# Attention with a gated MLP on one core: the half-size first product in step 0 of both blocks

## The chip, the cores and the metric

The kernel runs on one core of one Trainium2 chip. The time is device microseconds of one execution. Three runs of the kernel before gave 706.75, 707.27 and 707.87 us; the median, 707.27, is the time before.

The engines are called by the profile's names: PE is TensorE's matmul, PEld its weight load, DVE is VectorE, ACT is ScalarE, POOL is GpSimd, SP is SyncE, which here only issues DMAs.

## The reference

For x of 2048 x 1024 (bf16), with 32 heads of 32 and a hidden width of 3584:

```python
xn = _layernorm(x)
s = _A_ref(xn, A_wqkv, A_wo)           # attention of each position to 8 positions, 2 apart, then @ wo
g = _silu(_B_ref(xn, B_w1, B_w3, B_w2))
return x + s * g

def _B_ref(x, w1, w3, w2):
    gate = jnp.einsum("bsd,df->bsf", x, w1)
    up = jnp.einsum("bsd,df->bsf", x, w3)
    h = _silu(gate) * up
    return jnp.einsum("bsf,fd->bsd", h, w2)
```

## The kernel before

**Blocks, chunks, steps.** The 2048 rows are worked in two blocks of 1024, and each block in two chunks of 512 columns of the transposed x. A block goes through the q, k and v products (`qkv_pairs`), the gate/up steps (`up_step`, 14 of them, each for 256 of the 3584 hidden columns), the down product (`mlp_down`) and the output product (`wo`). The attention itself (`scores`, `softmax`, `values`) is DVE work that is spread between these. The output product of the first block's second chunk runs inside block 1, between its v products and its first steps; its output tile is stored from one of the six large buffers ("r8").

**Seven products for eight.** Each product is a 2 x 2 block product done with seven products instead of eight (the Strassen-Winograd form). For the gate/up step the four block operands of x are the two chunks times the two halves of the contraction (`bx`), their sums are `tx`, made once a block by `xn_sums` into the tile `xs`. The weights are blocked as gate (w1) and up (w3) times the two halves of the contraction; their four sums are made by `w_sums` (line 1307) in block 0, stored in DRAM (`s_dram`), and loaded again in block 1 as "st." (`up_load`, line 1216). A full product of a step is, for each of two groups of 128 hidden columns, four matmuls of 128x128 weights by 512 columns. `mm` (line 586) issues them at line 593.

**The half-size form.** The first of the seven products (w1's first half with the first chunk's first half) has no sums in it. In steps 1 to 13 it is itself done in the 2 x 2 form, with blocks of half the size: `up_first` (line 1267), seven pairs of matmuls of 256 columns, issued at line 1283. Its weight sums are made by `w_sums2` (line 1237: three DVE instructions named wss0, wss2 and wss3) in block 0, stored (`s2_dram`, POOL's queue) and loaded in block 1 ("s2.", SP's queue) into the part of the weight tile that w3's first half would take. Its x sums are made once a block by `x_sums2` (line 1253: four DVE instructions, named xt) into the place of xT's second chunk, first half, which nothing reads any longer. Between the pairs stand copies on ACT (`ufork`, `us5p`, `usnap`) and one DVE sum inside PSUM (`ucc`). `up_first` is a generator: `up_step` (line 1321) of the step before draws its four parts one after the other between its own products, so that the copies and the sum have time. The rows `L2F` (line 497) say which steps take this form; step 0 does not, since no step stands before it: it does the first product as two groups of four matmuls of 512 columns.

**What sets the order.** Nothing runs in program order. Every operation is first recorded with a cost and a due time (`Plan.op`). `Plan.listed` (line 254) makes a list for each engine from these, and then moves single operations by the table `ORDER` (line 328): a pair (a, b) takes operation a out and puts it right behind b; one row of the table for each of PE, DVE, ACT, POOL and SP. Each engine, and each DMA queue, then works strictly in its list's order, and waits for what its next operation needs. Operations are known in the table by their running number, so an added operation renumbers all behind it.

Vector sums are issued at line 602 (`tt`), copies at 607 (`cp`), silu at 624, DMAs at 634; the groups of the profile are told apart by their tiles and shapes. In the profile "r" is one of the six large buffers, "k" an SBUF tile for partial results, "mm" a PSUM bank, "a" an attention tile, "h_sb" the hidden activations.

Of the kernel before, what the change touches and what calls it, by code (L numbers as in the profile page):

```python
# [42 lines left out]
class Plan:  # L43
# [420 lines left out]
def kernel(  # L464
# [29 lines left out]
    L2B = (0, 1)  # L494
    LKB, EKB = 200, 200
    RL = (0,1,2)
    L2F = {0: range(1, 14), 1: range(1, 14)}
    KEEP = ('l1', 'l2')
    U2B = (0,1)
    CH_ = [r.split() for r in ("turn1_2_1 put_sq0_0", "ofork0_1 exp1", "u2_l10_1 sq2", "fk_l10_1 var2_1")]  # L500
# [806 lines left out]
    def w_sums(fb):  # L1307
# [9 lines left out]
        if U2B and fb:  # L1317
            w_sums2(fb)
# [780 lines left out]
```

## Time and profile before

| | us |
|---|---|
| median of 3 runs | 707.27 (706.75 to 707.87) |
| the profiled execution | 707.13 |
| its span, first to last instruction | 705.4 |
| PE busy | 696.8 |
| DVE busy | 676.4 |
| ACT busy | 385.4 |
| POOL busy | 40.6 |

The granted TensorE clock was 1.00 throughout. The span is 1.7 us shorter than the execution that it was taken from. Busy times say how much of the span an engine had an instruction in work; PE's are modelled, since its matmuls overlap. So the distance from one start to the next is the better measure of PE, and a list of waits the better measure of what held it. Times inside the profile are counted from the span's start. In this execution the first block's gate/up steps begin shortly after 81 us, and block 1's near 425 us.

### The profile page before, as it was taken

The page shows a single profiled execution, that of the slowest core. Times are in us where ns is not written, and L with a number is a line of the kernel's source. Part 1 is how long each engine was busy: PE and PEld are TensorE (multiplying, and loading weights), DVE is VectorE, ACT ScalarE, POOL GpSimd, SP SyncE. Part 2 cuts the span into 40 slices and gives each one's busy share as a digit, 9 for nine tenths or more (in the row PEclk, how much of TensorE's full clock was granted, in tenths as well). Part 3 has the DMA queues.
Part 4 walks back from the last instruction along what each step waited for, and adds up shares of the span by engine and source line. Part 5 has one row for each costly group of instructions (what it writes and reads, how often), then busy time and mean ns, then how long its engine had stood idle before and what let it go on. Part 6 is the DMA issues. An engine that isn't in the chain of part 4 may idle for free.

```text
span 705.4 us, 9790 instructions
## 1 busy us (share of the span) xinstructions
PE 696.8 (99%) x3611; PEld 374.5 (53%) x3666; DVE 676.4 (96%) x831; ACT 385.4 (55%) x752; POOL 40.6 (6%) x83
## 2 busy tenths in 40 slices
PE   9999999999999999999999999999999999999997
PEld 5555555545545474744555554454555555656443
DVE  8889999999999999999979999999999999999877
ACT  6644465658465796812564454566756755222143
POOL 1001020012101000000010000000100010000000
PEclk9999999999999999999999999999999999999999
DMA  9998889787788899996776767976675668858403
GB/s 333 291 354 305 300 290 319 256 271 268 227 300 291 300 287 212 300 270 215 266 240 237 238 212 225 306 240 217 204 237 177 199 187 251 270 210 268 153 28 119
DMA packets 142351, 174.06 MB, mean 247 GB/s; under 512 B 16912, under 2 KB 117280, under 8 KB 135648
## 3 DMA queue, kind: packets, MB, share of 16 engines
q1 hardware_dynamic: 131408, 138.10, 62.0%
q0 software_dynamic: 6240, 33.84, 12.8%
q10 hardware_dynamic: 4656, 1.51, 1.0%
q8 instruction: 28, 0.46, 0.3%
q14 instruction: 19, 0.16, 0.1%
HBM read 117.31 MB, written 43.78 MB: 228 GB/s over the span
## 4 chain that ended last, share of the span: by engine, by line
PE 94%; DVE 3%; DMA 2%; issue 1%; SPq 0%; ACT 0%; DVEq 0%; ACTq 0%
PE mm L593 82%; PE mm L1554 6%; PE mm L1283 5%; DMA r<-s_dram 1%; DVE r L602 1%; DVE a L602 1%; DMA r<-in_A_x_dram 1%; DMA out_dram<-r 1%; PE mm L781 0%; DVE small L699 0%; SPq L634 0%; DVE r L715 0%; DVE xT L602 0%; DVE E L602 0%; ACT k L607 0%
## 5 line engine op out<-in xcount | busy, mean ns | idle before, releaser
L593 PEld LDWEIGHTS <-r 128*128 128x128 f16 (+1 forms) x2068 | 219.6, 108 | 192.0 <-DMA r<-in_A_wqkv_dram 0.5
L593 PE MATMUL mm<-xs,r 128*128 128x512 f16 x1280 | 305.2, 379 | 0.3 <-DMA r<-s_dram 0.2
L593 PE MATMUL mm<-xT,r 128*128 128x512 bf16 (+2 forms) x747 | 177.6, 369 | 2.1
L607 ACT COPY k<-mm 128x512 f32<-128x512 f32 (+1 forms) x226 | 121.0, 565 | 74.0 <-PE mm L593 54.0
L607 ACT COPY mm<-mm 128x512 f32<-128x512 f32 (+1 forms) x157 | 75.6, 487 | 117.0 <-DVE mm L602 36.1
L593 PE MATMUL mm<-r,h_sb 128*128 128x512 f16 (+1 forms) x581 | 130.1, 379 | 0.6
L593 PEld LDWEIGHTS <-h_sb 128*128 128x128 f16 (+1 forms) x680 | 66.6, 98 | 78.4
L602 DVE TENSOR_TENSOR a<-a 128x2048 bf16<-128x2048 bf16 (+7 forms) x106 | 106.7, 1011 | 0.3
L602 DVE TENSOR_TENSOR h_sb<-mm,k 128x1024 bf16<-128x1024 f32 x48 | 58.2, 1217 | 7.1 <-PE mm L593 3.9
L1283 PE MATMUL mm<-xT,r 128*128 128x256 f16 (+1 forms) x364 | 61.1, 273 | 0.0
L602 DVE TENSOR_TENSOR a<-qo,kT 128x2048 bf16<-128x2048 bf16 x48 | 57.5, 1218 | 0.3 <-ACT kT L607 0.2
L602 DVE TENSOR_TENSOR h_sb<-h_sb 128x1024 f16<-128x1024 bf16 (+7 forms) x74 | 55.0, 748 | 0.2
L1283 PEld LDWEIGHTS <-r 128*128 128x128 bf16 (+1 forms) x364 | 35.6, 98 | 32.0
L602 DVE TENSOR_TENSOR a<-E,vT 128x2048 bf16<-128x2048 bf16 x42 | 50.3, 1217 | 0.3 <-issue 0.3
L602 DVE TENSOR_TENSOR k<-mm,k 128x1024 f32<-128x1024 f32 (+1 forms) x44 | 44.8, 1023 | 2.2 <-PE mm L593 2.1
L624 ACT ACTIVATE k<-k 128x512 bf16<-128x512 f32 x56 | 34.7, 636 | 15.5 <-DVE k L602 15.4
L602 DVE TENSOR_TENSOR r<-r,r 128x1024 f16<-128x1024 f16 (+7 forms) x56 | 42.5, 768 | 0.1
L624 ACT ACTIVATE h_sb<-mm 128x512 bf16<-128x512 f32 x60 | 36.2, 611 | 5.7 <-PE mm L593 5.5
L602 DVE TENSOR_TENSOR qo<-qo,a 128x2048 bf16<-128x2048 bf16 x32 | 39.0, 1219 | 0.3
L602 DVE TENSOR_TENSOR r<-r 128x1024 f16<-128x1024 bf16 (+4 forms) x71 | 36.1, 515 | 0.2
L602 DVE TENSOR_TENSOR h_sb<-h_sb,k 128x2048 bf16<-128x2048 bf16 x28 | 34.1, 1218 | 1.3 <-ACT k L607 1.2
L607 ACT CAST k<-mm 128x512 bf16<-128x512 f32 x56 | 32.3, 598 | 0.9 <-PE mm L593 0.7
(129 smaller groups left out, 528.9 us busy)
## 6 DMA issues: line engine op xcount, KB each, us to landing
r<-in_B_w_dram SPq DMA_DIRECT2D x42, 512.0 KB, 5.4
s_dram<-r POOLq DMA_DIRECT2D x14, 1024.0 KB, 5.2
r<-s_dram SPq DMA_DIRECT2D x14, 1024.0 KB, 5.7
r<-t_dram SPq DMA_DIRECT2D x15, 896.0 KB, 6.8
r<-in_A_wqkv_dram SPq DMA_DIRECT2D x10, 1024.0 KB, 8.6
r<-in_B_w_dram SPq DMA_DIRECT2D x11, 896.0 KB, 5.6
h_sb<-in_B_w_dram SPq DMA_DIRECT2D x14, 512.0 KB, 6.8
t_dram<-h_sb POOLq DMA_DIRECT2D x7, 1024.0 KB, 6.3
```

The source lines that it names most:

```text
L593: nc.tensor.matmul(cut(ps.ap()), lhsT=lhs[k](), rhs=cut(rhs[k]()), start=(first and k == 0), stop=(last and k == n - 1), skip_group_check= ...
L602: plan.op(DVE, name, lambda: fn(out=o(), in0=a(), in1=b()), rd, wr, occ, 0.08, late=late)
L607: plan.op(ACT, name, lambda: nc.scalar.copy(out=o(), in_=a()), rd, wr, occ, 0.11)
L624: plan.op(ACT, name, lambda: nc.scalar.activation(out=o(), in_=a(), func=ACTF.Silu), rd, wr, occ, 0.11, table="silu")
L1283: nc.tensor.matmul(half(pa[i].ap, n)(), lhsT=A[0][k](), rhs=B[0][k](), start=first and k == 0, stop=k == 1, skip_group_check=True)
L1554: nc.tensor.matmul(half(bank.ap, n)(), lhsT=a[k](), rhs=c[k](), start=first and k == 0, stop=k == NQ - 1, skip_group_check=True)
```

## The change

Step 0 of both blocks does its first block product in the half-size form, as steps 1 to 13 do. For that

- `L2F` takes in step 0;
- `up_step` of step 0 goes through `up_first` of its own step at once, before its other products are recorded;
- block 0 makes the weight sums of `w_sums2` for step 0 too, and stores them; block 1 loads them ("s2.0");
- `x_sums2` of block 0 is recorded ahead of `w_sums(0)` instead of behind it, with no other change; in block 1 it stays behind the scores;
- the table `ORDER` is another one for all five engines.

In the built kernel PE has 16 matmuls of 512 columns less and 28 of 256 more; DVE has 5 instructions more (three weight sums, two sums in PSUM), ACT 6 copies more, POOL one store and SP one load more. The lists that both kernels share differ in many places: 82 of PE's 907 shared operations stand out of their old sequence, 200 of DVE's 828, 234 of ACT's 727, 79 of SP's 259 and 22 of POOL's 70. PE's list is the same up to 57 us of the old trace and from 597 us on; DVE's and ACT's differ from 14 us to the end.

```diff
 ORDER = (
...
-    L2F = {0: range(1, 14), 1: range(1, 14)}
+    L2F = {0: range(0, 14), 1: range(0, 14)}
...
             dma(SP, f"w3.{fb}", lambda: wv()[:, 1, KH:KT], lambda: w3_r[:, KH:KT, fc], [], [(wt, 1, 1)], 256)
-            if b in U2B and fb:
+            if b in U2B:
                 dma(SP, f"s2.{fb}", lambda: s2_v(wt).rearrange("p q k n -> p (q k n)"),
                     lambda: s2_dram[fb].rearrange("p q k n -> p (q k n)"), [("sd2", fb)], [(wt, 1, 0)], 256)
...
-        if U2B and fb:
+        if U2B:
             w_sums2(fb)
...
         more = up_first(b, fb + 1) if fb + 1 in L2F[b] else iter(())
+        if two and not fb:
+            for _ in up_first(b, fb):
+                pass
         pa, pe, pb = [PA[b, fb] if two and x == "a" else banks(*(f"u{x}{b}_{fl[i]}" for i in I)) for x in "aeb"]
...
         if b == 0:
+            x_sums2()
             w_sums(0)
...
         if b:
             scores(c0)
-        if b in U2B:
+        if b:
             x_sums2()
```

In the changed lists, PE's last quarter of block 0's new product stands behind the first product with sums of step 0 (`ue0`) and ahead of the last v products. The sum `ucc` that it needs stands on DVE right behind the second pair sum of the v products (`qc22`). In block 1, DVE's new `ucc` stands among the sums of the first block's second output chunk, and SP's stores of that chunk stand in another sequence.

262 rows, old and new, of the table ORDER are left out of this document.

## The prediction

> **What bounds the kernel now.** I read the page's first lines, then what TensorE (PE) waits for, then the chain of waits, because the change touches PE work and the question is whether PE time is the kernel's time.
>
> ```profile
> span 705.4 us, 9790 instructions
> ...
> PE 696.8 (99%) x3611; PEld 374.5 (53%) x3666; DVE 676.4 (96%) x831; ACT 385.4 (55%) x752; POOL 40.6 (6%) x83
> ```
>
> ```profile
> PE mm L575 <- DVE k L573: 1.3, 1, 1.3
> PE mm L781 <- DVE r L715: 0.3, 1, 0.3
> PE mm L593 <- DMA r<-s_dram: 0.2, 1, 0.2
> ```
>
> PE is busy 99%, VectorE (DVE) 96%. A busy PE is a modelled figure, so the second fence matters more: in the whole execution only three waits of PE are listed, 1.8 us in all, and two of them are in the first microseconds. The chain of waits tells how fast PE issues when nothing holds it; its columns are start, length and what, with the count of matmuls:
>
> ```profile
> 630.31 3.02 PE mm L593 x14
> 633.33 7.64 PE mm L1554 x70
> ```
>
> 14 matmuls of 512 columns in 3.02 us are 215.7 ns each; 70 of 256 columns in 7.64 us are 109.1 ns each. So PE is a full queue with hardly a hole, and work taken from it shortens the kernel one for one, unless something else then arrives last. Two things might: DVE, and one DMA.
>
> DVE first. The columns of the windows are the stretch, its length, then busy time and instruction count of PE, PEld, DVE, ACT and POOL, then clock, DMA share and GB/s.
>
> ```profile
> 50.50:83.60 33.10, 32.94 (x152) 18.94 (x154) 32.49 (x36) 13.41 (x26) 2.12 (x4) 1.00 0.85 301
> 58.00:362.00 304.00, 302.79 (x1574) 161.93 (x1596) 301.69 (x395) 183.44 (x347) 24.96 (x47) 1.00 0.84 272
> 410.00:452.00 42.00, 41.74 (x204) 20.83 (x205) 41.76 (x49) 21.77 (x46) 1.09 (x2) 1.00 0.76 239
> ```
>
> In the first block, 58 to 362 us, DVE is busy 301.69 of 304 us: it works off a backlog, and what PE needs is merely placed early enough in it. The backlog is empty for the first time at 362 us, where DVE idles 3.12 us:
>
> ```profile
> 361.95 0.42 DVE L602 TENSOR_TENSOR xT<-xT 128x512 f16<-128x512 bf16 x1
> 365.49 1.23 DVE L602 TENSOR_TENSOR h_sb<-mm,k 128x1024 bf16<-128x1024 f32 x1 [3.12 <-ACT k L607]
> ```
>
> The DMA is the third wait of PE, and the chain shows what stands behind it:
>
> ```profile
> 436.34 1.14 DVE a L602
> 437.48 0.61 DVE r L602
> ...
> 439.54 3.61 DMA out_dram<-r
> ...
> 443.20 8.90 DMA r<-s_dram
> ...
> 452.15 3.63 PE mm L593 x16
> ```
>
> ```profile
> 451.35 0.60 PE L1283 MATMUL mm<-xT,r 128*128 128x256 f16 x4
> 452.15 1.04 PE L593 MATMUL mm<-xs,r 128*128 128x512 f16 x4 [0.20 <-DMA r<-s_dram]
> ```
>
> In block 1 the load of step 2's weight sums (st.2) needs a buffer that holds the output of the first block's second chunk. The last sums of that output leave DVE at 438.09, the last of its stores is issued at 439.54 and lands at 443.15, then the load takes 8.90 us. PE's four half matmuls of 451.35 end their issue at 451.35 + 4 x 0.109 = 451.79, and PE starts again at 452.15: it stands still for 0.36 us. Whatever PE gains before 452 us counts only as far as st.2 comes sooner too.
>
> **The change, part by part.** *PE work.* In each block's step 0 two accumulations of four 512-column matmuls go, 8 per block, 16 in all; seven pairs of 256-column matmuls come, 14 per block, 28 in all. 16 x 215.7 = 3.451 us against 28 x 109.1 = 3.055 us: 0.40 us less, half of it in each block. The Trainium skill, page "TensorE: Matmul & The Clock Gate", section "Back-to-back issue gap", speaks against this: it gives streams of weight load and matmul about 81 ns for 128 columns and 131 ns for 512. By that (estimate) 28 half products would cost at least 28 x 81 = 2.27 us against 16 x 131 = 2.10, a loss of 0.17 us or more; the trace disagrees with its 215.7 ns, so the measurement decides.
>
> *DVE.* Three new weight sums for step 0 (block 0 only: block 1 loads them), and one combining sum in PSUM per block.
>
> ```profile
> 83.54 1.28 DVE L602 TENSOR_TENSOR r<-r 128x1024 f16<-128x1024 bf16 x2
> ...
> 85.88 0.41 DVE L602 TENSOR_TENSOR r<-r 128x512 f16<-128x512 bf16 x1
> 86.22 1.21 DVE L602 TENSOR_TENSOR a<-a 128x2048 bf16<-128x2048 bf16 x1
> 87.35 0.28 DVE L602 TENSOR_TENSOR r<-r 128x256 f16<-128x256 bf16 x1
> 87.55 1.21 DVE L602 TENSOR_TENSOR a<-a 128x2048 bf16<-128x2048 bf16 x1
> ...
> 95.97 0.68 DVE L602 TENSOR_TENSOR mm<-mm,k 128x512 f32<-128x512 f32 x1
> 96.57 0.41 DVE L602 TENSOR_TENSOR r<-r 128x512 f16<-128x512 bf16 x1
> ```
>
> From start to next start the same sums of step 1 take 0.34, 0.20 and (same form) 0.20 us, the combining sum 0.60. So block 0 gets 0.74 + 0.60 = 1.34 us more and block 1 0.60 us. Over block 0 the 1.34 us fit the 3.12 us hole at 362 us; without that cover they would cost 1.34. The x sums are only moved: the same four instructions.
>
> *Step 0 of block 0 itself.* Now the last quarter of the half-size product waits for the combining sum. On DVE, in the order of the changed kernel, it stands right behind the second sum of the v products, after which the next instruction starts at 83.54 today; ahead of that sum stand the same instructions plus the three weight sums. So it starts between 83.54 + 0.74 = 84.28 and, if the idle 33.10 - 32.49 = 0.61 us closes, 83.67, and gives its result 0.69 us later: 84.36 to 84.97. PE:
>
> ```profile
> 81.56 1.67 PE L593 MATMUL mm<-xT,r 128*128 128x512 bf16 x7
> 83.07 2.75 PE L593 MATMUL mm<-xs,r 128*128 128x512 f16 x12
> ```
>
> The old product ends at 83.07 (8 matmuls, one record missing), the eight behind it 1.73 us later, 84.80. In the changed order the same work stands ahead of the last quarter, less 8 x 0.2157 plus 12 x 0.1091: 84.38. So PE stalls 0 to 0.6 us. I take 0, the near end, since DVE's idle time there is mostly waiting for PE sums that now have other work in front; 0.6 stays in the range. Behind the waiting matmul stands all of PE, so the price is full.
>
> *ScalarE* gets three 256-column copies per block. Each takes about as long as this group's mean (the third number):
>
> ```profile
> L607 ACT COPY mm<-mm 128x256 f32<-128x256 f32 x69 | 25.5, 370 | 34.6 <-PE mm L1283 27.5 <-PE mm L1554 6.9
> ```
>
> ScalarE is busy 13.41 of 33.10 us in that stretch: 1.1 us fit. Between the quarters stand v-product matmuls of 0.86 us or more, which hide copy and hand-over. Cost 0; without that cover at most 0.4 us per hand-over, two per block.
>
> *DMA.* A 256 KB store in block 0 on POOL's queue (POOL is busy 2.12 of 33.10 us) and a 256 KB load in block 1 on SP's, placed between the first weight load and st.0:
>
> ```profile
> 412.89 0.38 SPq L634 DMA_DIRECT2D r<-in_B_w_dram  x1
> 415.87 0.34 SPq L634 DMA_DIRECT2D park_v<-h_sb  x1
> ```
>
> SP's queue is free from 413.27 to 415.87, so its 0.4 us of issue cost nothing. What it takes from the transfers beside it I can't see: 0 to 1 us at st.2, and I take 0, since it lands long before st.2 starts.
>
> *Other orders.* They decide st.2. DVE last idles before it at 414 us, for a sum that PE has to deliver:
>
> ```profile
> 414.62 1.22 DVE L602 TENSOR_TENSOR h_sb<-mm,k 128x1024 bf16<-128x1024 f32 x1 [0.24 <-PE mm L593]
> ```
>
> From there to the output's last sum DVE is full. In the changed order, ahead of that last sum stand the new combining sum (0.60) and one score addition of 128x2048 more (1.14, the 436.34 row): 1.74 us. Against it, one output subtraction is drawn ahead of 414 us and fills the 0.24 us of idle there, and block 0 brings PE there 0.2 us sooner, which helps as far as DVE can follow. That leaves 438.09 + 1.74 - 0.24 = 439.59, or 439.39 with the 0.2. The stores stand in another order too: today the last is issued 1.45 us after the last sum, behind other stores and a load that wait their turn in SP's queue; in the changed order the store with the last data is the last store, so it goes out at once. So its issue moves from 439.54 to between 439.39 and 439.59, and st.2 with it; I take **0.1 us sooner**. The rest of PE's 0.4 us ends in a longer wait there, about 0.36 + 0.3 = 0.66 us.
>
> **Sum.** The profiled execution took 707.13 us (span 705.4 and 1.7 around it); minus 0.1 is 707.0. The median of the runs is 0.14 above that execution: **707.2 us**, no difference that a measurement of this kernel can tell; it can tell about 0.2%, 1.41 us.
>
> **Rivals.**
> - *PE gets everything.* st.2 comes early enough and PE loses neither the 0.36 us nor anything new: 707.27 - 0.40 - 0.36 = 706.5. For it: the orders are new everywhere. Against: the DVE count above. To pass 705.86 (0.2%) another 0.65 us would have to come from the starting stretch, where PE waits 1.6 us.
> - *DVE is late in step 0.* The 0.6 us above, in block 0: 707.27 - 0.40 + 0.6 = 707.5.
> - *st.2 becomes the bound and comes late (slower).* The 1.74 us on DVE aren't made up and the store queue saves nothing: st.2 starts 1.74 later, and PE with it: 709.0. A slower landing would do the same:
>
> ```profile
> park_k<-h_sb SPq DMA_DIRECT2D x1, 1024.0 KB, 10.7
> ```
>
> st.2 lands in 8.9 us, this transfer of the same size in 10.7, 1.8 more. For it: this wait has no cover, so it decides from the first tenth; +0.2% is passed when st.2 starts later than 443.2 + 1.4 = 444.6. Against it: the new order of the stores.
>
> Were DVE the bound throughout, its 1.94 us would be paid in full: 707.27 - 0.40 + 1.94 = 708.8. The 3.12 us hole speaks against that in block 0, and in block 1 it is the st.2 case; I count it there.
>
> **How the numbers follow.** Forecast 0.63; PE gets everything 0.14, of which 0.05 passes 705.86; DVE late 0.10; slower case 0.13. Faster 0.05, same 0.63 + 0.09 + 0.10 = 0.82, slower 0.13. The range goes from 706.5 less the runs' own scatter of 0.6 (706.75 to 707.87) to 707.5 plus the unknown 1 us of the transfers: 705.9 to 708.6.
>
> **What would show it.** Right: PE's groups of L593 with 16 fewer matmuls of 512 and L1283 with 28 more of 256; the chain with st.2 issued near 443.1 and PE again held there, for longer than 0.36 us; no PE wait for the DVE sum near 84 us; DVE's hole at 362 us shrunk by some 1.3 us. Wrong: a new wait of PE on DVE or ScalarE in either step 0, a chain that no longer passes through st.2, or a hole at 362 us that is gone while PE waits after it.

## The result and the profile after

Six executions of the changed kernel took 709.85 us in the median (708.74 to 711.01), beside six of the kernel before with 707.13 (706.75 to 707.87): the ratio is 1.0038, 95% interval 1.0025 to 1.0051. The change makes the kernel slower, by about 2.7 us; the forecast was 707.2 and its upper end 708.6. The profiled execution took 709.08 us, 1.95 more than the one before.

The first lines of the page of after:

```profile
span 707.3 us, 9833 instructions
...
PE 696.6 (98%) x3623; PEld 375.7 (53%) x3678; DVE 678.0 (96%) x836; ACT 385.6 (55%) x758; POOL 41.2 (6%) x84
```

All lines of code behind the change have moved by 4 (the products by 4 to 7). PE has 12 matmul records more, as 28 for 16 gives, and is busy 0.2 us less while the span is 1.9 us longer. So PE does no more work; it stands still more. What it waits for in after:

```profile
PE mm L1561 <- ACT mm L611: 1.4, 2, 1.1
PE mm L579 <- DVE k L577: 1.3, 1, 1.3
PE mm L785 <- DVE r L719: 0.8, 2, 0.5
PE mm L1287 <- ACT k L611: 0.3, 1, 0.3
```

The wait for the load st.2 (DMA r<-s_dram) that the forecast turned on is gone. Two waits on ScalarE are new. The second and third line lie in the first microseconds, as before. The larger of the new ones is in block 0's down product, PE's timeline of after (start, length, what, in brackets the idle time before it):

```profile
280.81 1.46 PE L597 MATMUL mm<-r,h_sb 128*128 128x512 f16 x6
282.36 0.93 PE L1561 MATMUL mm<-r,xs 128*128 128x256 f16 x7
...
286.93 1.67 PE L597 MATMUL mm<-r,h_sb 128*128 128x512 f16 x7
289.75 1.69 PE L1561 MATMUL mm<-r,xs 128*128 128x256 f16 x14 [1.15 <-ACT mm L611]
291.72 3.22 PE L1561 MATMUL mm<-r,xs 128*128 128x256 f16 x28 [0.28 <-ACT mm L611]
```

The brackets count from a modelled end, so I take the starts. Seven matmuls from 286.93 are issued by 286.93 + 7 x 0.2157 = 288.44; the next starts at 289.75: PE stands for **1.31 us**. In the same way 0.26 us at 282.10, 0.44 at 291.28 and 0.09 at 294.77: 2.10 us in this stretch. PE waits there for a SiLU and for copies that ScalarE makes inside PSUM (fk_l20_0 and fk_l20_1, one for each group). ScalarE's timeline of after shows why these are late:

```profile
267.71 1.41 ACTq L808 DMA_TRANSPOSE xT<-r  x1
...
270.44 8.77 ACTq L808 DMA_TRANSPOSE xT<-r  x3
279.26 1.06 ACT L730 ACTIVATE r<-r 128x1024 bf16<-128x1024 bf16 x1 [8.85 <-issue]
...
280.42 1.28 ACT L628 ACT_TABLE_LOAD   x1
281.72 0.60 ACT L628 ACTIVATE xs<-mm 128x512 bf16<-128x512 f32 x1
...
282.40 0.60 ACT L628 ACTIVATE xs<-mm 128x512 bf16<-128x512 f32 x1
...
289.31 0.38 ACT L611 COPY mm<-mm 128x256 f32<-128x256 f32 x1
```

And the same stretch of before:

```profile
261.24 1.05 ACT L726 ACTIVATE r<-r 128x1024 bf16<-128x1024 bf16 x1
...
268.86 1.28 ACT L624 ACT_TABLE_LOAD   x1
272.69 0.60 ACT L624 ACTIVATE xs<-mm 128x512 bf16<-128x512 f32 x1 [2.55 <-PE mm L593]
272.76 1.44 ACTq L804 DMA_TRANSPOSE xT<-r  x1
...
274.45 3.52 ACTq L804 DMA_TRANSPOSE xT<-r  x1
278.01 0.60 ACT L624 ACTIVATE xs<-mm 128x512 bf16<-128x512 f32 x1 [3.60 <-issue]
...
285.94 0.36 ACT L607 COPY mm<-mm 128x256 f32<-128x256 f32 x1
```

Here ScalarE issues four DMA transposes of block 1's normalized rows (turn2_0 to turn2_3). In after nothing else starts on it while it issues the last three, 8.77 us. Both kernels are let go at about the same time, 278.0 and 279.2. The difference is what stands behind that point, ahead of the copy. In before the row sum `mean3_1` stands at 261.24, ahead of the transposes, and the table load and the SiLU `dg#3` (silu of the down product's output) between them. In after all three stand behind: 289.31 - 279.26 = 10.05 us of work ahead of the copy, against 285.94 - 278.01 = 7.93. (The three are 1.05 + 1.28 + 0.60 = 2.93 us; the difference is smaller, 2.12, since the rest of the stretch isn't the same work in both.)

The smaller wait is in steps 2 to 5 of block 0. VectorE and PE of after:

```profile
97.40 0.69 DVE L606 TENSOR_TENSOR h_sb<-h_sb 128x1024 f16<-128x1024 bf16 x1 [0.74 <-issue]
```

```profile
103.17 1.03 PE L597 MATMUL mm<-xT,r 128*128 128x512 bf16 x4
104.50 0.38 PE L1287 MATMUL mm<-xT,r 128*128 128x256 f16 x2 [0.30 <-ACT k L611]
```

VectorE stands for 0.74 us ahead of this instruction. It (`w2s#20`, a sum of down weights) needs the load `w2q#11`, which lands at 97.32 by the trace; the profile doesn't name what it waited for. PE then stands 0.46 us at 104.04, 0.10 at 108.6 and 0.20 at 120.6: 0.76 us. The load's place on SyncE and GpSimd, from after and then from before:

```profile
83.44 2.17 SPq L638 DMA_DIRECT2D h_sb<-in_B_w_dram  x3
```

```profile
86.33 1.07 POOL L638 DMA_DIRECT2D s_dram<-r  x2 [21.46 <-DVE r L606]
```

```profile
81.96 1.60 SPq L634 DMA_DIRECT2D h_sb<-in_B_w_dram  x3
```

```profile
89.86 0.53 POOL L634 DMA_DIRECT2D s_dram<-r  x1 [21.12 <-DVE r L602]
```

The three loads of 512 KB are w2q 8, 9, 11 in after and 11, 9, 8 in before. In before all have landed by 89.55, ahead of the store of step 0's weight sums at 89.86. In after the weight sums are ready sooner, the store of 1 MB starts at 86.33 with the new store of 256 KB behind it, and the third load takes 12.2 us.

At st.2, PE's and SyncE's timelines of after:

```profile
445.11 0.33 SPq L638 DMA_DIRECT2D r<-s_dram  x1
```

```profile
453.79 0.60 PE L1287 MATMUL mm<-xT,r 128*128 128x256 f16 x4
454.23 2.11 PE L597 MATMUL mm<-xs,r 128*128 128x512 f16 x9
```

453.79 + 4 x 0.109 = 454.23: no wait. PE comes 2.4 us later than before and the load, which lands at 452.95, is there.

In sum PE stands 2.10 + 0.76 = 2.86 us in after behind the first 12 us, and 0.36 in before; with 0.40 us of work less that makes 2.86 - 0.36 - 0.40 = 2.1 us. The profiled executions differ by 1.95, the medians by 2.72; the 0.6 us between the sum and the medians aren't explained, and after's six runs scatter by 2.3 us.

### The profile page after: what moved, and what is told of

Same layout as the page of the kernel before. It is cut to its first block, busy times and chain, and to the rows that moved or that the text cites. A ratio compares the mean times of both kernels' runs of the same rounds, so it can differ in the third digit from the quotient of the medians.

```text
span 707.3 us, 9833 instructions
## 1 busy us (share of the span) xinstructions
PE 696.6 (98%) x3623; PEld 375.7 (53%) x3678; DVE 678.0 (96%) x836; ACT 385.6 (55%) x758; POOL 41.2 (6%) x84
## 4 chain that ended last, share of the span: by engine, by line
PE 90%; ACT 3%; DMA 2%; DVE 2%; ACTq 1%; issue 1%; SPq 0%; DVEq 0%
PE mm L597 79%; PE mm L1287 6%; PE mm L1561 5%; DMA h_sb<-in_B_w_dram 2%; ACTq L808 1%; ACT r L747 1%; ACT k L735 1%; DVE small L703 0%; DMA r<-in_A_x_dram 0%; ACT mm L611 0%; SPq L638 0%; DVE h_sb L606 0%; DVE a L606 0%; ACT r L730 0%; PE mm L785 0%
## 5 line engine op out<-in xcount | busy, mean ns | idle before, releaser
L597 PE MATMUL mm<-xT,r 128*128 128x512 bf16 (+2 forms) x731 | 175.1, 369 | 2.1
L611 ACT COPY mm<-mm 128x512 f32<-128x512 f32 (+1 forms) x161 | 77.6, 486 | 132.6 <-DVE mm L606 45.6
L606 DVE TENSOR_TENSOR a<-a 128x2048 bf16<-128x2048 bf16 (+7 forms) x106 | 108.2, 1023 | 0.4
L1287 PE MATMUL mm<-xT,r 128*128 128x256 bf16 (+1 forms) x392 | 64.9, 273 | 0.3 <-ACT k L611 0.3
L1287 PEld LDWEIGHTS <-r 128*128 128x128 bf16 (+1 forms) x392 | 38.3, 98 | 33.7 <-issue 0.6
L606 DVE TENSOR_TENSOR r<-r 128x1024 f16<-128x1024 bf16 (+3 forms) x74 | 37.9, 521 | 0.5 <-DMA xT<-r 0.4
```

Source lines behind the costliest of these rows:

```text
L597: nc.tensor.matmul(cut(ps.ap()), lhsT=lhs[k](), rhs=cut(rhs[k]()), start=(first and k == 0), stop=(last and k == n - 1), skip_group_check= ...
L606: plan.op(DVE, name, lambda: fn(out=o(), in0=a(), in1=b()), rd, wr, occ, 0.08, late=late)
L611: plan.op(ACT, name, lambda: nc.scalar.copy(out=o(), in_=a()), rd, wr, occ, 0.11)
L1287: nc.tensor.matmul(half(pa[i].ap, n)(), lhsT=A[0][k](), rhs=B[0][k](), start=first and k == 0, stop=k == 1, skip_group_check=True)
```

## The experiments

Eleven kernels, each beside runs of the kernel before on the same chip (medians 707.06 to 707.33); runs 1 to 4 are from one chip, 5 to 11 from another. "Lists" are the engines' orders.

| kernel | median us (range) | ratio to before, 95% |
|---|---|---|
| 1 after, mean3_1 and dg#3 earlier | 706.86 (706.31 to 707.86) | 0.9992 (0.9983 to 1.0001) |
| 2 after, w2q#11 earlier | 708.97 (708.23 to 710.43) | 1.0030 (1.0020 to 1.0039) |
| 3 after, both | 706.67 (706.12 to 707.34) | 0.9991 (0.9982 to 1.0000) |
| 4 after, old lists | 708.97 (708.09 to 709.81) | 1.0024 (1.0014 to 1.0034) |
| 5 before, new lists | 709.58 (708.76 to 710.05) | 1.0035 (1.0022 to 1.0047) |
| 6 before, mean3_1 and dg#3 later | 708.09 (707.81 to 709.16) | 1.0016 (1.0007 to 1.0025) |
| 7 before, w2q#11 later | 707.24 (706.71 to 708.23) | 1.0004 (0.9995 to 1.0013) |
| 8 after, new store later | 709.51 (708.31 to 709.93) | 1.0034 (1.0021 to 1.0046) |
| 9 after, dg#3 alone earlier | 708.18 (706.99 to 709.28) | 1.0012 (1.0004 to 1.0021) |
| 10 after, mean3_1 alone earlier | 707.09 (706.32 to 708.41) | 0.9995 (0.9986 to 1.0004) |
| 11 before, new lists with both mends | 707.37 (706.96 to 709.12) | 1.0001 (0.9993 to 1.0010) |

The theory: the new lists cost the time, at two places, and the half-size step costs nothing. The rival: the half-size step costs it by its own sums, copies and transfers.

**1. Two instructions earlier on ScalarE's list.**

```diff
 dfork0_3
+mean3_1
 dfork0_2
...
 turn2_2
+dg#3
 turn2_3
 turn2_0
-mean3_1
 dg#2
 halov
-dg#3
 mean3_0
```

> The changed kernel with two instructions moved on ScalarE's list and nothing else: the x3 row sum mean3_1 goes from behind the four turn2 transposes to ahead of them (behind dfork0_3), and the SiLU dg#3 from behind them to between turn2_2 and turn2_3, about where the kernel before has both. Theory (the list is late): ScalarE has 1.05 + 1.28 (table load) + 0.6 = 2.9 us less to do between the last transpose and the copy fk_l20_0, so the copy ends near 286.8 and not 289.70, before TensorE asks for it at 288.44; the four TensorE stalls of 0.26, 1.31, 0.44 and 0.09 us at 282 to 295 go, and the time falls from 709.85 by 1.7 to 2.1 us, to 707.8 to 708.2. Rival (the half-size step costs that time by its own copies, sums and store, and the stalls only show it): the stalls come up elsewhere and the time stays at 709.4 to 710.2. A third way: the wait for the load st.2 at 452, gone in the changed kernel since TensorE comes late, comes back with 0.3 to 0.9 us, and the time is 708.3 to 708.8.

The time falls to 706.86, further than expected. No stall of PE is left from 282 to 295, those at 105 to 122 stay (0.43, 0.09, 0.20 us), and none comes up at st.2. From the end of the last product ahead of the stretch ("da0") to the end of the first behind it ("de0", both of the down product) PE needs 36.39 us here and 38.48 in after: 2.09 less, the whole sum of the four stalls. The rest of the difference of the medians (about 0.9 us) is in no stretch that I can name: the runs of after scatter by 2.3 us, and the profile shows one of them. Executions differ by such amounts from the start: in the profiled one of run 1, the longest of its eleven, PE waits 1.14 us for the first weights, and its matmuls of 256 columns begin at 12.89 us, where after has 11.89. The rival is out: nothing of the half-size step was touched.

**2. One load earlier on SyncE's list.**

```diff
 w1.2
+w2q#11
 w2q#8
 w2q#9
-w2q#11
```

> The changed kernel with one load moved on SyncE's list: w2q#11 is issued ahead of w2q#8 and w2q#9, as in the kernel before, and nothing else. Theory (the load's place costs it): it lands near 90 and not at 97.32, VectorE's wait of 0.74 us ahead of w2s#20 at 96.66 goes, TensorE's stalls of 0.46, 0.10 and 0.20 us at 104, 109 and 121 go, and the time falls by 0.5 to 0.8 us, to 709.1 to 709.35; the load that is now last, w2q#9, lands near 97.3 and is asked for only at 99.3. Rival (VectorE is late by the added sums, 0.74 + 0.60 us, not by the load): the wait goes, the stalls stay within 0.2 us and the time within 0.3 us of 709.85.

VectorE's timeline of this kernel:

```profile
96.74 0.69 DVE L606 TENSOR_TENSOR h_sb<-h_sb 128x1024 f16<-128x1024 bf16 x1
```

The row has no bracket: the wait is gone (w2q#11 lands at 89.55, w2q#9 now at 97.17), and PE has no stall left from 12 to 281 us. But PE then comes to the other place sooner, and the SiLU holds it there for 0.62 us where it was 0.26. So of 0.76 us 0.40 are left, and the median falls by 0.9, which the intervals of the two ratios, 1.0025 to 1.0051 and 1.0020 to 1.0039, don't tell from nothing; the trace carries this one. The wait was the cause of the three stalls; the added sums alone were not, since they are all still there.

**3. Both.**

> Both moves of the two runs before in one kernel. Theory: the gains add, 1.7 to 2.1 and 0.5 to 0.8 us, and the time is 707.0 to 707.6, about the time of the kernel before. Rival (the half-size step itself costs about 2 us): not below 709. If st.2 at 452 comes back into play, 707.4 to 708.2.

706.67, below the 707.0 to 707.6 expected and the shortest of all, 0.9991 of before (0.9982 to 1.0000): a gain on before at the edge of what these runs can tell. All waits of PE in this kernel:

```profile
PE mm L579 <- DVE k L577: 1.2, 1, 1.2
PE mm L785 <- DVE r L719: 0.2, 1, 0.2
```

Behind the first 11 us PE never stands still. This is the kernel that the forecast's "PE gets everything" rival priced at 706.5. SyncE issues st.2 here, where before does so at 443.20:

```profile
441.86 0.33 SPq L638 DMA_DIRECT2D r<-s_dram  x1
```

That is 1.34 us sooner: the last store ahead of it leaves 0.48 us sooner (439.06 against 439.54) and lands in 2.68 us where before's takes 3.61. The load itself takes 7.41 us where before's takes 8.90. It lands at 449.27, and PE comes to it 2.0 us later, at 451.27.

**4. The half-size step with the old lists.** All shared instructions in the order of before, except from 70 to 82 and from 422 to 438 us, where the new products need the new order.

> The changed kernel's instructions with the lists of the kernel before, except inside the two first steps (70 to 82 and 422 to 438 us), where the new products need the new order; the new store and the new load stand where the changed kernel has them among their neighbours. Theory (the half-size step is worth its 0.4 us of TensorE and costs nothing, the other lists cost the rest): 706.7 to 707.3, at or a little below the kernel before. Rival (the half-size step costs by its copies, sums and transfers): 708.0 to 710.

The theory's number failed, by 1.7 us, and the rival's range holds the time. PE in this kernel, at block 0's step 0 and at st.2:

```profile
83.30 1.89 PE L597 MATMUL mm<-xs,r 128*128 128x512 f16 x8
85.30 0.38 PE L1287 MATMUL mm<-xT,r 128*128 128x256 f16 x2
85.52 1.02 PE L597 MATMUL mm<-xs,r 128*128 128x512 f16 x4
86.83 1.02 PE L597 MATMUL mm<-xT,r 128*128 128x512 bf16 x4 [0.28 <-ACT mm L611]
...
454.96 2.33 PE L597 MATMUL mm<-xs,r 128*128 128x512 f16 x10 [1.19 <-DMA r<-s_dram]
```

None of the larger stalls of after is here. Instead the last quarter of the new product waits 0.28 us for its sum on VectorE (85.30 - 83.30 - 8 x 0.2157), the full product behind it 0.45 for a copy, block 1's last quarter 0.26, a product of its step 1 0.52, and st.2, issued at 446.38 and not at 443.20, holds PE for 1.35. There is also a wait of 0.23 us at 75.7. These are waits of the kinds that the forecast's second and third rival name, 0.28 us (up to 0.6 there) and 1.35; that the time, 708.97, is near the third's 709.0 is luck, since the other waits are in it as well. With these lists, then, the step's own sums and copies do hold PE, as the rival has it. The lists that the change came with have none of these waits; they bring two others. My lists cross from one order to the other inside the first steps, so how much of the 0.28 to 0.52 us is from the seams stays open; the wait at st.2 is 15 us away from one.

**5. The new lists without the half-size step.**

> The kernel before (full-size first product in step 0 of both blocks, no new sums, copies, store or load) with the changed kernel's lists on every engine: all shared instructions stand in the changed kernel's order, the four full-size products where the neighbours have them. Theory (the lists cost the time, whatever the product's size): the TensorE stalls at 282 to 295 of about 2.1 us come up without the half-size step, perhaps the 0.5 to 0.8 us near 104 to 121 too, and the time is 708.6 to 709.9. Rival (the half-size step costs it by its own work on VectorE, ScalarE and the queues): 707.0 to 707.6.

709.58, as slow as after (1.0035 against 1.0038), with the same stalls, 0.73, 1.31, 0.45 and 0.09 us, on the old work. There are none at 104 to 121: the new store is missing there, w2q#11 lands at 94.83, and VectorE has the three weight sums less. So the large place comes from the lists alone; the small one needs the lists and the added work or store together.

**6. The kernel before with the two ScalarE instructions late.**

```diff
 dfork0_3
-mean3_1
 dfork0_2
...
 turn2_0
-dg#3
 nrm2_2
 turn2_3
 turn2_2
+mean3_1
 dg#2
 halov
+dg#3
 var3_2
```

> The kernel before with only the two ScalarE instructions put where the changed kernel has them: mean3_1 from behind dfork0_3 to behind the last transpose turn2_2, dg#3 from between the transposes to behind halov. Theory (these two places are the whole cause of the stalls at 282 to 295): the work ahead of fk_l20_0 grows by 2.9 us, its end goes from 286.30 to about 289.2 where TensorE asks at 288.4, fk_l20_1 from 288.12 to about 291; TensorE stalls 0.8 to 1.9 us there, the 0.36 us at st.2 go in return, and the time is 707.9 to 708.9. Rival (other list changes of that stretch are needed as well): within 0.3 us of the kernel before.

In size as expected, 1.0 us; the place is another one. PE here:

```profile
273.82 3.40 PE L593 MATMUL mm<-r,h_sb 128*128 128x512 f16 x15
278.39 0.92 PE L1554 MATMUL mm<-r,xs 128*128 128x256 f16 x7 [1.17 <-ACT xs L624]
```

PE's list of before asks for the result of dg#3 first, so the whole stall, 278.39 - 273.82 - 15 x 0.2157 = 1.33 us, falls on the SiLU, and the copies are in time again. The expectation also had PE ask for the first copy at 288.4, which is after's time; before asks at 287.64. These two places on one list are enough to make the old kernel slower.

**7. The kernel before with w2q#11 as the last of the three loads.**

```diff
 w3.2
-w2q#11
 w2q#9
 w2q#8
+w2q#11
```

> The kernel before with only the load w2q#11 moved on SyncE's list behind w2q#9 and w2q#8, as the changed kernel has it. Theory (the place costs nothing by itself; it costs because the changed kernel's two stores of weight sums start at 86.33 and 86.85, ahead of its landing): here the store starts only at 89.86, the load lands near 90 as the last of the three did, VectorE asks at 91.9, no wait, 707.0 to 707.6. Rival (the place alone): a VectorE wait ahead of w2s#20 and 0.5 to 0.8 us more time.

707.24, no difference, and no wait of PE behind the first 11 us. So the place in the list by itself costs nothing.

**8. The new store behind the next one.**

```diff
 s_dram#0
-s2_dram (step 0)
 s_dram#1
+s2_dram (step 0)
```

> The changed kernel with only the new store (s2_dram of step 0) moved on GpSimd's queue behind the store s_dram#1, so that it starts at about 94 and not at 86.85. Theory (the new store is what w2q#11 shares the queues with): the load lands 2 to 4 us sooner, before VectorE asks at 96.66, the wait of 0.74 us and the stalls of 0.76 us go, 709.0 to 709.4. Rival (the store s_dram#0, earlier by 3.5 us, does it alone): the load still lands behind 96.7 and the time stays within 0.3 us of 709.85.

The theory's 2 to 4 us didn't come: the load still lands at 97.32, 11.7 us after its issue (12.2 in after; 10.1 in run 5, which has no new store), and VectorE still waits, 0.30 us by its timeline; the stall at 104 is gone, those at 109 and 121 stay, the time is 709.51. The rival holds for the landing, while the 0.46 us at 104 go with the new store's place: w2q#11 lands some 0.5 us behind the store of 1 MB here (96.83), 0.3 us behind it in run 5 (94.56) and 1.2 us in after (96.12). That this store delays it fits all of these and run 7, but it was not taken away by itself: a later load needs the tile that it stores.

**9 and 10. The two ScalarE instructions one by one.** The edits are the halves of run 1.

> The changed kernel with only the SiLU dg#3 moved on ScalarE's list, to between turn2_2 and turn2_3; mean3_1 stays behind the transposes. The table load of 1.28 us goes with the first SiLU, so by the theory 1.88 us of the 2.9 us leave the stretch: dg#2 ends near 281.0 (asked 282.1), fk_l20_0 near 287.8 (asked 288.44), fk_l20_1 near 289.8 (asked 289.96); all four stalls at 282 to 295 go, 707.0 to 707.9. Rival (both moves are needed): 0.5 us or more of stalls stay there, 708.0 to 709.0.

> The changed kernel with only the row sum mean3_1 moved ahead of the transposes; dg#3 and the table load stay behind them. By the theory 1.05 us leave the stretch: dg#2 ends near 281.3 (no stall), fk_l20_0 near 288.65 against 288.44 asked (0.2 us), fk_l20_1 near 290.6 against 290.2 (0.4 us): 0.5 to 0.8 us of the 2.1 us stay, 707.6 to 708.5. Rival (the row sum is the cause, the SiLU is not): no stall there, 707.0 or less.

Both missed their theories, the other way round: 708.18 with the SiLU alone, 707.09 with the row sum alone. By itself run 9 reads as "both moves are needed"; run 10 shows that the row sum's is enough. ScalarE in run 9, then in run 10:

```profile
271.00 3.38 ACTq L808 DMA_TRANSPOSE xT<-r  x1
274.42 1.28 ACT L628 ACT_TABLE_LOAD   x1 [3.44 <-issue]
274.48 1.71 ACTq L808 DMA_TRANSPOSE xT<-r  x1
...
276.23 4.17 ACTq L808 DMA_TRANSPOSE xT<-r  x1
280.44 1.06 ACT L730 ACTIVATE r<-r 128x1024 bf16<-128x1024 bf16 x1 [4.14 <-issue]
```

```profile
272.35 6.57 ACTq L808 DMA_TRANSPOSE xT<-r  x3
278.95 1.28 ACT L628 ACT_TABLE_LOAD   x1 [6.63 <-issue]
```

I had taken the end of the transposes as fixed. Counted from the end of the same PE product ahead of them (260.95 us in after, 261.48 in run 9, 261.85 in run 10, 261.83 in run 1), ScalarE is let go 18.3 us later in after, 18.9 in run 9, 17.1 in run 10 and 17.3 in run 1. With the row sum ahead of them the transposes are issued later and end 1 us sooner; three of them in a row took 6.57 us and not 8.77. So the row sum is worth its own 1.05 us and 1.2 us of the transposes' time, and alone takes all four stalls away. The SiLU alone wins 1.88 us of work and loses 0.6 at the transposes; seven short waits of PE for ScalarE and VectorE stay between 285 and 299 us, 1.13 us together. Why the transposes end sooner isn't settled: the trace shows when each was issued and landed, not what held it. One thing goes with it: in after and run 9 the first transpose is issued 0.5 us behind a load on SyncE's queue (267.71 and 267.19 in after) and lands after 7.2 and 7.3 us, and the second one's issue takes 3.3 and 3.4 us; in runs 1 and 10 it is issued 1.6 us behind that load and lands after 5.6 and 5.5 us, and the second one's issue takes 1.9 and 1.8. No run changes this distance by itself, so it isn't shown to be the cause.

**11. Full-size products, new lists, both mends.** Run 3 without the half-size step.

> The kernel before (full-size first products) with the changed kernel's lists and the mends of both: mean3_1, dg#3 and w2q#11 at their early places. Against the run with both mends and half-size products (706.67) the size of the product is then all that differs, with its sums, copies, store and load. Theory (TensorE is the bound and nothing holds it, so the 0.40 us of matmul time come through whole): 706.9 to 707.4, and no TensorE stall over 0.3 us behind 12 us. Rival (the half-size step is worth nothing): 706.4 to 706.8. Another rival: a TensorE wait at st.2 or in a first step that the half-size product had cured: above 707.5.

707.37 against 706.67: 0.70 us. The two runs are from two chips, and the intervals of their ratios to before overlap (0.9993 to 1.0010, 0.9982 to 1.0000), so the traces have to tell the parts. From the end of the v products to the end of step 1's first sums PE needs 24.63 us here and 24.43 in run 3: 0.20 for block 0. The same over block 1's steps 0 and 1: 33.08 and 32.85, 0.23. One wait of 0.24 us at 339 us is this kernel's own. So the half-size step is worth its 0.40 us by the traces, and with these lists PE gets all of it. Run 5, with the same work and the same lists without the mends, took 709.58: on this chip the three moves are worth 2.2 us without any half-size product.

## Why the prediction was wrong

- **What bounds the kernel: right.** PE's time is the kernel's time wherever nothing holds it; run 3 has no hold at all and is the shortest.
- **PE work, -0.40 us: right**, 0.20 and 0.23 us in the two blocks by the traces of runs 3 and 11. With it the estimate from the Trainium skill's page "TensorE: Matmul & The Clock Gate", "Back-to-back issue gap", a loss of 0.17 us, is out for this kernel.
- **DVE, +1.34 us covered by the hole at 362 us: the cost was right, the cover was not.** From start to next start the three weight sums take 0.33, 0.20 and 0.20 us in after and the combining sum of block 0 takes 0.60. But the hole is as long in run 3 as in run 11, 2.78 us both times:

```profile
365.18 1.23 DVE L606 TENSOR_TENSOR h_sb<-mm,k 128x1024 bf16<-128x1024 f32 x1 [2.78 <-ACT k L611]
```

```profile
365.81 1.23 DVE L602 TENSOR_TENSOR h_sb<-mm,k 128x1024 bf16<-128x1024 f32 x1 [2.78 <-ACT k L607]
```

  The sums go into short waits of VectorE that were spread over the block: from 58 to 362 us it is busy 302.61 us in run 3 and 301.35 in run 11. Run 11's timeline has three of these waits, all for PE, 1.05 us together; run 3 has none of them:

```profile
79.97 1.23 DVE L602 TENSOR_TENSOR h_sb<-mm,k 128x1024 bf16<-128x1024 f32 x1 [0.47 <-PE mm L593]
...
94.58 1.23 DVE L602 TENSOR_TENSOR h_sb<-mm,k 128x1024 bf16<-128x1024 f32 x1 [0.27 <-PE mm L593]
...
106.91 1.23 DVE L602 TENSOR_TENSOR h_sb<-mm,k 128x1024 bf16<-128x1024 f32 x1 [0.31 <-PE mm L593]
```

- **Step 0 of block 0, 0 of 0 to 0.6 us: right** for the lists that came with the change: in after the combining sum starts at 83.55, ends at 84.24, and PE comes to the last quarter at 84.37 (84.38 in the forecast). With other lists (run 4) it was 0.28.
- **ScalarE's three copies per block, 0: right** for the copies themselves: no stall lies in either step 0 of after or run 3.
- **DMA, "0 to 1 us at st.2, and I take 0": right at st.2, wrong place.** The stores were weighed where block 1's load lies. In block 0 the two stores are under way beside w2q#11, which lands behind both, and PE loses 0.76 us there. The load's new place is needed for that (run 2) and does nothing in the old kernel (run 7); the new store's place goes with the first stall, 0.46 us (run 8); the part of the 1 MB store isn't shown by itself.
- **"Other orders. They decide st.2": this is the step that failed.** I read the new orders at this one place, since it was the one where PE waited before, and gave the other moved instructions (234 on ScalarE alone) no price; "something else then arrives last" was looked for on DVE and one DMA only. The place that decided, ScalarE's list around the four transposes, was quoted nowhere, and it held PE for 2.10 us. What would have warned of it stands in the trace of before: fk_l20_0 ends at 286.30, and PE asks for it at 287.64:

```profile
287.64 4.75 PE L1554 MATMUL mm<-r,xs 128*128 128x256 f16 x42
```

  So the slack is 1.3 us, while 1.05 us of row sum, 1.28 of table load and 0.60 of SiLU, 2.93 us, are moved behind the transposes. That comparison is a warning and not yet a price: run 10 keeps 1.88 us of this behind them without a stall, since there the transposes end sooner. The second place, w2q#11, had no price either, and cost 0.76 us.

  At st.2 itself the forecast was off too. It moved the last store's issue by 0.1 us, left the landings as they were, and had PE wait 0.66 us. In run 3, where nothing else makes PE late, st.2 is issued 1.34 us sooner, its load is 1.49 us shorter, and PE doesn't wait at all.
- **Sum and rivals.** The slower case was named with st.2 and had 709.0; what came was of this size but by another mechanism, so that nearness is luck. The range didn't even hold this rival: it ends at 708.6 (707.5 and 1 make 708.5), although 709.0 had a chance of 0.13. Run 4 shows a wait of 1.35 us at st.2, but with other lists. Of the signs, the chain that no longer passes through st.2 did come, and stood under "wrong"; the wait of PE on ScalarE came too, but in block 0's down product and not in a step 0; the hole at 362 us, 2.78 us in after, said nothing. The list of PE's waits was the sign to watch.

## What to carry to other kernels

Where a change comes with new orders, look at every instruction that passes a long blocking one on an in-order engine, not only at those near the old critical wait: look up the slack between the end of the result behind it and the time at which its consumer asks for it, in the trace before, and compare it with the work that is moved in front. Don't take the end of the blocking instructions as fixed: here a row sum of 1.05 us, put ahead of four transposes instead of behind them, won ScalarE 2.2 us, and a SiLU with its table load, put between them, won it 1.88 us and lost 0.6 at the transposes. And a cost of the lists can be told from a cost of the work by building both kernels with both lists: here the step was worth 0.40 us, and moving two instructions and one load back took away all 2.86 us of waits.

## What the hardware showed

- In this kernel ScalarE, which issues the DMA transposes from its own queue, is held by them for long and varying times: three in a row 8.77 us in after, 6.57 in run 10. With 1.05 us more work ahead of them (run 10) they ended 1.2 us sooner, and not later.
- The table load takes 1.28 us, and can run beside the issue of a transpose that stands behind it: in run 9 it starts at 274.42 and the next transpose's issue at 274.48. The Trainium skill, page "ScalarE: Activation LUTs", section "What ACT_TABLE_LOAD costs", has the same 1.28 us but adds 1.38 for a drain at every switch; in after the instruction ahead ends at 280.41, the load runs from 280.42 and the SiLU starts at 281.72, so this trace shows no such drain on either side.
- Three loads of 512 KB one behind the other landed 6.2, 6.6 and 12.2 us after their issue in after, where a store of 1 MB began 1.2 us behind the issue of the last; in run 7, where that store began 6.8 us behind it, the last took 6.4 us.
